# Operand forms in a split-precision MoE kernel: weights at other offsets and in steps, one moving operand in steps, one phase with its columns backwards

## The chip, the cores and the metric

The kernel runs on one core of one Trainium2 chip. The metric is the device time of one execution in microseconds, as the median of several runs. The core has a matrix engine (TensorE: matmuls, and the loads of their weights), a vector engine (VectorE), a scalar engine (ScalarE), GpSimd, and DMA queues, issued here by SyncE. In the profile the engines are PE (with PEld for the weight loads), DVE, ACT, POOL and SP.

## The reference

Sigmoid attention over 8 batches, 12 heads, 448 tokens and 64 dimensions a head, and on its output a two-layer network with a gated activation.

```python
def _attn_ref(q, k, v):
    S = q.shape[2]
    scale = 1.0 / np.sqrt(q.shape[-1])
    scores = scale * np.matmul(q, k.transpose(0, 1, 3, 2)) - np.log(S)
    attn = 1.0 / (1.0 + np.exp(-scores))
    return np.matmul(attn, v).astype(np.float32)

def _moe_ref(x, w_in, w_out):            # x: 3584 x 768, w_in: 768 x 2048, w_out: 2048 x 768
    h = x @ w_in
    relu6 = np.clip(h + 3.0, 0.0, 6.0)
    g = h * relu6 / 6.0
    return (g @ w_out).astype(np.float32)
```

The weights come to the kernel as 8-byte numbers (float64 bits seen as pairs of int32) and are decoded to float32 on the chip.

## The kernel before, in words

The work has three parts in a row on TensorE.

*Attention.* Scores (L200) and attention times values (L217), in quarter-array matmuls of 64 x 64 weights and 448 columns. The other engines meanwhile decode the weights (`decode`, L48 to L66: it reads and writes the low and the high halves of 8-byte numbers, so every second int32) and store them to DRAM.

*The first product, x @ w_in.* It and the second product are done as Strassen-like block products (Winograd's form): seven products M1 to M7 in place of eight, of sums and differences of the quarters of each matrix. `WEIGHT` and `MOVING` name which quarter, or which sum, each product takes as weights and as moving operand. Tokens are taken in four pairs of batches (p = 0 to 3). Each float32 operand is split into a rounded part and a remainder, both in the type float32r (`split`, L69: ScalarE writes the rounded part, VectorE the remainder), and each product of blocks is three matmuls: high by high, high by low, low by high. `w1_split` (L304) splits the weights of one slot: slot n, of 112, has one tile `w_n` of the ring, 128 partitions by two parts of 768 floats, which starts `SHIFT_1` = 48 floats into its buffer. `product` (L362) runs 18 matmuls on it, each with 128 x 128 weights and 448 moving columns. In profiles its rows are L376, with outputs A, B and D.

*The second product, g @ w_out.* The list `units` holds 56 units: for each product in the order of `PHASES` (M1, M2, M6, M7, M5, M4, M3), for each pair p, and for each half h of the inner dimension, one unit of 36 matmuls (three blocks of output rows, four blocks of the inner dimension, three matmuls each; rows of L676, output po). Eight units with the same weights make a phase. Per unit, VectorE forms a difference where the phase needs one (`g_sum`, in M5 and M4), and `g_split` (L479) splits the moving operand into the tile `gx`; this is done two units ahead. `w2_split` (L489) splits a phase's weights, three tiles for each h, of 128 partitions by two parts of 512 floats, `SHIFT_2` = 8 floats into their buffers, one unit ahead. `post2` reads the finished sums. Stores, loads and reloads go through SyncE's queue.

All four engines' orders are written out by the program itself (a manual schedule); the tables `at_slot`, `at_unit` and `at_fetch` set at which slot or unit a step is issued.

The three places where operands get their form:

```python
        w = ring(f"w_{n}", [P, 4 * KW + 64], F32R)[:, SHIFT_1 : SHIFT_1 + 4 * KW]        # w1_split
        gx[n] = gset[n % 3].tile([P, 2, FC, S], F32R, tag="gx", name=f"gx_{n}")          # g_split
            w2[i, h, ec] = w.rearrange("p (t c e) -> p t c e", t=2, c=FC)                # w2_split
```

In all of them each row of 128 weights, or of 448 moving columns, lies in one piece, in rising order, and starts at a multiple of 32 bytes.

Of the kernel before, what the change touches and what calls it, by code (L numbers as in the profile page):

```python
# [9 lines left out]
F32R = mybir.dt.float32r  # L10
# [6 lines left out]
B, H, S, D = 8, 12, 448, 64  # L17
DM, DF = 768, 2048
P = 128
# [6 lines left out]
FC = DF // P // 4  # L26
KW = KC * P
# [5 lines left out]
SHIFT_1, SHIFT_2 = 48, 8  # L33
# [6 lines left out]
M1, M2, M3, M4, M5, M6, M7 = range(7)  # L40
# [2 lines left out]
B11, B21, B22, T4, T1, T2, T3, B12 = range(8)  # L43
MOVING = {M1: B11, M2: B21, M3: B22, M4: T4, M5: T1, M6: T2, M7: T3}
PHASES = (M1, M2, M6, M7, M5, M4, M3)


def decode(nc, st, a):  # L48
# [20 lines left out]
def split(nc, hi, lo, a):  # L69

    nc.scalar.copy(hi, a)  # L71
    yield
    nc.vector.tensor_tensor(out=lo, in0=a, in1=hi.bitcast(F32), op=ALU.subtract)  # L73
    yield
# [20 lines left out]
def tile_kernel(ctx: ExitStack, tc: tile.TileContext, qk, vP, wi, wo, outT):  # L95
    nc = tc.nc
# [44 lines left out]
    def ring(name, shape, dtype):  # L141
        return dw.tile(shape, dtype, tag="ring", name=name, bufs=5)
# [21 lines left out]
    def at_unit(n, f, *a):  # L164
        plan.setdefault(n, []).append((f, a))
# [125 lines left out]
    for u in range(4 * EC):  # L291
        kh, ec = divmod(u, EC)
# [9 lines left out]
            nc.sync.dma_start(out=wst[n], in_=dw1[q % NQ][:, WEIGHT[i]])  # L302

    def w1_split(n):  # L304
        w = ring(f"w_{n}", [P, 4 * KW + 64], F32R)[:, SHIFT_1 : SHIFT_1 + 4 * KW]
        wr[n] = w.rearrange("p (t j c f) -> p t j c f", t=2, j=2, c=KC)
        flat = w.rearrange("p (t n) -> p t n", t=2)
        yield from split(nc, flat[:, 0], flat[:, 1], wst.pop(n).rearrange("p j n -> p (j n)"))
# [10 lines left out]
    for n in range(LA):  # L319
        on(NS - 10 + n, w1_load, n)  # L320
        gen = w1_split(n)
        over(on, (NS - 3 + n,), gen)
        over(on_late, (NS - 2 + n,), gen)
# [127 lines left out]

    units = [(i, p, h) for i in PHASES for p in range(NPR) for h in range(2)]
    gset, gr, gs, gx = [], {}, {}, {}
# [6 lines left out]
    def g_load(n):  # L460
        if n < len(units):
            i, p, h = units[n]
            first, _ = PARTS.get(MOVING[i], (MOVING[i], None))
            gr[n] = gset[n % 3].tile([P, FC, S], F32, tag="gr", name=f"gr_{n}")
            nc.sync.dma_start(out=gr[n], in_=gd[p, first, h])

    def g_load2(n):
        if n < len(units) and MOVING[units[n][0]] in PARTS:
            i, p, h = units[n]
            gs[n] = [ring(f"gr_{n}_{k}", [P, 2, S], F32) for k in range(2)]  # L470
            for k in range(2):
                nc.sync.dma_start(out=gs[n][k], in_=gd[p, PARTS[MOVING[i]][1], h][:, 2 * k : 2 * k + 2])

    def g_sum(n):
        for k, o in enumerate(gs.pop(n, ())):
            part = gr[n][:, 2 * k : 2 * k + 2]
            nc.vector.tensor_tensor(out=part, in0=part, in1=o, op=ALU.subtract)  # L477

    def g_split(n):  # L479
        gx[n] = gset[n % 3].tile([P, 2, FC, S], F32R, tag="gx", name=f"gx_{n}")  # L480
        yield from split(nc, gx[n][:, 0], gx[n][:, 1], gr.pop(n))

    w2s, w2 = {}, {}
# [5 lines left out]
    def w2_split(i, h):  # L489
        st, gens = w2s.pop((i, h)), []  # L490
        for ec in range(EC):
            w = xs.tile(
                [P, KC * S], F32R, tag="xT" if h else "xraw", name=f"w2_{i}_{h}_{ec}", bufs=3 if h else 5
            )[:, SHIFT_2 : SHIFT_2 + 2 * FC * P]
            flat = w.rearrange("p (t n) -> p t n", t=2)
            w2[i, h, ec] = w.rearrange("p (t c e) -> p t c e", t=2, c=FC)
            gens.append(split(nc, flat[:, 0], flat[:, 1], st[:, ec]))
        for _ in range(2):
            for g in gens:
                next(g)  # L500
            yield
# [14 lines left out]
    for n in range(LA, end):  # L516
        over(at_slot, (n - LA, n - LA + 1), w1_split(n))
    for h in range(2):
        at_slot(end - 22 + 7 * h, w2_load, M1, h)
        over(at_slot, (end - 20 + 7 * h, end - 19 + 7 * h), w2_split(M1, h))  # L520
# [9 lines left out]
    at_slot(last[M6, p_last] + 1, xt_close, B11, T2)  # L530
    at_slot(last[M6, p_last] + 1, g_load, 0)
    over(at_slot, (last[M6, p_last] + 3, last[M6, p_last] + 4), g_split(0))
    at_slot(last[M2, p_last] + 1, xt_close, T3, B21)
    at_slot(last[M2, p_last] + 1, g_load, 1)
    over(at_slot, (end, end), g_split(1))
    for n, (i, q) in enumerate(seq):
        for f, a in later.pop(n, []):
# [38 lines left out]
    for h, n in ((0, 0), (1, 8)):  # L576
        for e in range(2 * EC):
            k, ec = divmod(e, EC)
# [8 lines left out]
        at_unit(n + 2 * EC + 2, w2_store, h, S4)  # L587
    for k, i in enumerate(PHASES[1:]):
        n = 8 * (k + 1)
        for h in range(2):  # L590
            if (i, h) == (M6, 1):
                at_unit(n, w2_direct, i, h)
            else:
                at_fetch(n - 2 + h, w2_load, i, h)
            over(at_unit, (n - 1 + h, n - 1 + h), w2_split(i, h))
# [10 lines left out]
    po, so = {}, {}  # L606
# [14 lines left out]
    def post2(i, p, n):  # L621
        t = po.pop(p)
        if n < len(units) - 1:
            t = t[:, :, :S]
        if i == M1:
            so[p] = kept(i, p)
            nc.scalar.mul(so[p], t, SIXTH)
        elif i == M6:
            stt(so[p], t, so[p])
        elif i == M7:  # L630
            so["u3", p] = kept(i, p)
            stt(so["u3", p], t, so[p])
        else:
            eh, k, other = {M2: (0, 0, p), M5: (1, 1, ("u3", p)), M4: (1, 0, ("u3", p)), M3: (0, 1, p)}[i]
            o = out_tile(i, p)
            if n == len(units) - 1:
                for ec in range(EC):
                    stt(o[:, ec], t[ec], so[other][:, ec])
                    nc.sync.dma_start(out=outT[2 * p + k, eh * EC + ec], in_=o[:, ec])
                return  # L640
            stt(o, t, so[other])
            if i == M5:
                stt(so[p], t, so[p])
            at_unit(n + 1, put, p, eh, k, o)

    for n, (i, p, h) in enumerate(units):
        if n == 0:
            for _ in range(2):
                for f, a in later.pop(min(later)):
                    f(*a)  # L650
        elif n == 1:
            while later:
                for f, a in later.pop(min(later)):
                    f(*a)
            tmp_ctx.close()
            acc_ctx.append(ctx.enter_context(tc.tile_pool(name="acc", bufs=1, side="right", reuse_waits="tile")))
        for f, a in fetch.pop(n, []):
            f(*a)
        g_load2(n + 3)
        g_load(n + 4)  # L660
        for f, a in plan.pop(n, []):
            f(*a)
        if n + 2 < len(units):
            g_sum(n + 2)
            for _ in g_split(n + 2):
                pass
        if h == 0 and n == len(units) - 2:
            po[p] = [po_pool.tile([P, 512], F32, tag="pl" if ec < 2 else "po", name=f"pl_{ec}")[:, :S] for ec in range(EC)]
        elif h == 0:
            po[p] = po_pool.tile([P, EC, 512], F32, tag="po", name=f"po_{i}_{p}")  # L670
        x = gx.pop(n)
        for ec in range(EC):
            w = w2[i, h, ec]
            for c in range(FC):
                for wk, xk in ((0, 0), (0, 1), (1, 0)):
                    nc.tensor.matmul(  # L676
                        po[p][ec] if n > len(units) - 3 else po[p][:, ec, :S],
                        w[:, wk, c],
                        x[:, xk, c],
                        start=h == 0 and c == 0 and xk == 0 and wk == 0,  # L680
                        stop=h == 1 and c == FC - 1 and wk == 1,
                    )
        if h == 1:
            post2(i, p, n)
# [34 lines left out]
```

## Time and profile before

| | |
|---|---|
| median of 3 runs | 1074.76 us (1074.35 to 1074.85) |
| the profiled execution | 1075.04 us, span 1073.2 us |
| TensorE busy, matmuls | 1065.8 us, 99% of the span |
| TensorE busy, weight loads | 891.7 us, 83% |
| VectorE, ScalarE, GpSimd busy | 750.0, 561.6, 174.2 us |
| granted TensorE clock | 1.00 |
| DMA queues | 276 MB, 73% of the 16 engines' time |

A group's row gives its line, engine and operation, tiles and shapes and count; then its busy time in us, the mean of one in ns, the idle time of the engine just before its instructions, and what ended most of that. Matmuls are pipelined: the mean of one is longer than the distance between two.

### The profile page before, as it was taken

How to read it: one execution, taken by the hardware profiler on the slowest of the kernel's cores; microseconds unless marked ns; L12 is line 12 of the kernel's file. 1: busy time of each engine (PE TensorE's matmuls, PEld its weight loads, DVE VectorE, ACT ScalarE, POOL GpSimd, SP SyncE). 2: the span in 40 equal slices, each digit the busy share in tenths (PEclk: the TensorE clock that was granted, in tenths of full speed). 3: DMA queues.
4: the chain of work that ended last, by engine and by line, in shares of the span. 5: the costliest groups of instructions: out<-in, count | busy, mean ns of one | idle time of the engine just before them, and what ended most of it. 6: DMA issues, size and time to landing. Idle time of an engine off the chain costs nothing.

```text
span 1073.2 us, 16721 instructions
## 1 busy us (share of the span) xinstructions
PE 1065.8 (99%) x6784; PEld 891.7 (83%) x6784; DVE 750.0 (70%) x713; ACT 561.6 (52%) x612; POOL 174.2 (16%) x82
## 2 busy tenths in 40 slices
PE   9999999999999999999999999999999999999998
PEld 4444556666999999999999999999999999999998
DVE  4679855652677989898988665987864447787642
ACT  7889978886455644665465555434322313222420
POOL 0214230000143236333522221200000000000000
PEclk9999999999999999999999999999999999999999
DMA  8887998873776887779766778878885376898741
GB/s 307 295 323 271 336 362 291 317 276 128 251 252 206 248 280 226 237 229 317 225 216 214 276 248 283 299 265 306 339 315 194 109 276 223 286 345 286 271 149 52
DMA packets 81484, 277.13 MB, mean 258 GB/s; under 512 B 7936, under 2 KB 22272, under 8 KB 81408
## 3 DMA queue, kind: packets, MB, share of 16 engines
q1 hardware_dynamic: 81408, 276.07, 73.3%
q8 instruction: 53, 0.87, 0.3%
q14 instruction: 23, 0.19, 0.0%
HBM read 189.92 MB, written 86.11 MB: 257 GB/s over the span
## 4 chain that ended last, share of the span: by engine, by line
PE 85%; DVE 7%; DMA 3%; ACT 2%; issue 2%; SPq 0%; ACTq 0%; DVEq 0%
PE po L676 26%; PE A L376 21%; PE D L376 11%; PE sc L200 10%; PE pv L217 10%; PE B L376 5%; ACT gx L71 2%; DVE gr L477 2%; PE pl L676 1%; DMA qk<-qk 1%; DMA gr<-gd 1%; DMA dw<-w2S 1%; DVE w L73 1%; DVE gx L73 1%; DVE o L610 0%
## 5 line engine op out<-in xcount | busy, mean ns | idle before, releaser
L676 PE MATMUL po<-gx,w 128*128 128x448 f32 x1944 | 390.0, 362 | 0.6 <-DVE w L73 0.4
L676 PEld LDWEIGHTS po<-gx,w 128*128 128x128 f32 x1944 | 364.1, 187 | 26.4 <-DVE w L73 1.4
L376 PE MATMUL A<-x,w 128*128 128x448 f32 x1152 | 236.1, 362 | 0.4 <-DVE w L73 0.4
L376 PEld LDWEIGHTS A<-x,w 128*128 128x128 f32 x1152 | 215.8, 187 | 15.8 <-DVE w L73 0.7
L71 ACT CAST gx<-gr 128x1792 fp32r<-128x1792 f32 x56 | 94.8, 1694 | 205.0 <-PE po L676 102.4
L200 PE MATMUL sc<-qk 64*64 64x448 f32 x1344 | 197.4, 537 | 1.9 <-DMA qk<-qk 1.0
L217 PE MATMUL pv<-a,v 64*64 64x448 f32 x1344 | 197.1, 536 | 0.0
L202 ACT ACTIVATE a<-sc,bias_s 128x896 f32<-128x896 f32 x168 | 168.6, 1011 | 43.8 <-PE sc L200 39.8
L73 DVE TENSOR_TENSOR w<-ws,w 128x768 fp32r<-128x768 f32 x112 | 155.5, 1397 | 24.9 <-ACT w L71 24.9
L73 DVE TENSOR_TENSOR gx<-gr,gx 128x1792 fp32r<-128x1792 f32 x56 | 113.3, 2024 | 77.2 <-ACT gx L71 77.1
L200 PEld LDWEIGHTS sc<-qk 64*64 64x64 f32 x1344 | 70.3, 133 | 62.8 <-issue 28.3
L217 PEld LDWEIGHTS pv<-a,v 64*64 64x64 f32 x1344 | 71.3, 133 | 59.1 <-issue 38.0
L376 PE MATMUL D<-x,w 128*128 128x448 f32 x576 | 120.3, 362 | 0.0
L71 ACT CAST w<-ws 128x768 fp32r<-128x768 f32 x112 | 93.0, 830 | 43.5 <-DMA ws<-dw 43.4
L376 PEld LDWEIGHTS D<-x,w 128*128 128x128 f32 x576 | 108.0, 187 | 7.2
L228 DVE TENSOR_TENSOR xr<-pv,y 128x448 f32<-128x448 f32 x48 | 29.9, 624 | 79.8 <-ACT y L227 79.8
L410 POOL TENSOR_TENSOR gT<-g,g 128x896 f32<-128x896 f32 x16 | 43.5, 2721 | 258.2 <-DVE g L387 167.1
L376 PE MATMUL B<-x,w 128*128 128x448 f32 x288 | 60.3, 362 | 0.0
L376 PEld LDWEIGHTS B<-x,w 128*128 128x128 f32 x288 | 53.9, 187 | 4.3 <-issue 0.7
L396 ACT ACTIVATE g<-cD,bias 128x896 f32<-128x896 f32 x32 | 33.5, 1047 | 40.8 <-DVE cD L405 24.7
L401 ACT COPY u<-A 128x896 f32<-128x896 f32 x32 | 29.0, 906 | 39.0 <-PE A L376 39.0
L387 DVE SCALAR_TENSOR_TENSOR g<-g,cD 128x896 f32<-128x896 f32 x32 | 43.2, 1351 | 6.3 <-ACT g L396 6.3
(65 smaller groups left out, 766.9 us busy)
## 6 DMA issues: line engine op xcount, KB each, us to landing
gr<-gd SPq DMA_DIRECT2D x56, 896.0 KB, 5.6
ws<-dw SPq DMA_DIRECT2D x112, 384.0 KB, 4.2
gd<-g SPq DMA_DIRECT2D x64, 448.0 KB, 4.8
qk<-qk SPq DMA_DIRECT2D x48, 448.0 KB, 7.1
gd<-gT SPq DMA_DIRECT2D x32, 448.0 KB, 5.2
gr<-gd SPq DMA_DIRECT2D x32, 448.0 KB, 6.0
wi<-wi SPq DMA_DIRECT2D x16, 768.0 KB, 8.4
wo<-wo SPq DMA_DIRECT2D x24, 512.0 KB, 4.5
```

The costliest lines, as they stand in the source:

```text
L71: nc.scalar.copy(hi, a)
L73: nc.vector.tensor_tensor(out=lo, in0=a, in1=hi.bitcast(F32), op=ALU.subtract)
L200: nc.tensor.matmul(out, k[halves[r], at_k], q[halves[r]], start=True, stop=True)
L202: nc.scalar.activation(a, sc[:, :, :S], AF.Sigmoid, bias=bias_s, scale=scale)
L217: nc.tensor.matmul(pv[p][halves[j], r, :S], v, a[halves[r], int(r != j) if c is None else j], start=first, stop=last)
L228: nc.vector.tensor_tensor(out=xr[b, u][:, k], in0=pv[p][:, 1, :S], in1=y, op=ALU.add)
L376: nc.tensor.matmul(t[:, j, :S], w[:, wk, j, kc], x[:, xk, kc], start=i in (M1, M2, M5) and m == 0, stop=m == 3 * KC - 1, skip_group_check= ...
L387: nc.vector.scalar_tensor_tensor(out=r, in0=r, scalar=6.0, in1=h, op0=ALU.min, op1=ALU.mult)
L396: nc.scalar.activation(r, h, AF.Relu, bias=bias_3, scale=1.0)
L401: nc.scalar.copy(acc[key, q], acc["A", q][:, :, :S])
L410: nc.gpsimd.tensor_tensor(out=t3, in0=quad[q, B22], in1=quad[q, B12], op=ALU.subtract)
L676: nc.tensor.matmul(po[p][ec] if n > len(units) - 3 else po[p][:, ec, :S], w[:, wk, c], x[:, xk, c], start=h == 0 and c == 0 and xk == 0 an ...
```

## The change

Some operands of the two products get another form in SBUF or PSUM, each form in a stretch of its own:

- First product: the weights of slot n start n // 14 floats further on. Slots 0 to 13 stay as they are, the next 14 start 4 bytes on, and so on to 28 bytes for the last 14. Each slot has 18 matmuls.
- Second product, phase M6: the weights' tile has its order changed so that the two parts of a weight lie side by side; a row of 128 weights is read in steps of 8 bytes.
- Phase M5: the four inner blocks lie side by side; a row of 128 weights is read in steps of 16 bytes.
- Phase M7, pair 0 alone (units 24 and 25, 72 matmuls): the two parts of the moving operand lie side by side; 448 columns are read in steps of 8 bytes.
- Phase M2: the moving operand's columns are read backwards, and the outputs are written backwards in PSUM, so that each column comes to its old place.

The splits by ScalarE and VectorE write in the new forms, with as many elements and instructions as before. The order of the instructions on every engine is the same before and after; only the listed shape of M6's and M5's weight splits reads 128x4x128 in place of 128x512.

```diff
+BACKWARD = (M2,)
+WEIGHT_FORM = {M6: "p (c e t) -> p t c e", M5: "p (t e c) -> p t c e"}
+INTERLEAVED = (M7, 0)
...
     def w1_split(n):
-        w = ring(f"w_{n}", [P, 4 * KW + 64], F32R)[:, SHIFT_1 : SHIFT_1 + 4 * KW]
+        o = SHIFT_1 + n // 14
+        w = ring(f"w_{n}", [P, 4 * KW + 64], F32R)[:, o : o + 4 * KW]
...
     def g_split(n):
-        gx[n] = gset[n % 3].tile([P, 2, FC, S], F32R, tag="gx", name=f"gx_{n}")
+        t = gset[n % 3].tile([P, 2 * FC * S], F32R, tag="gx", name=f"gx_{n}")
+        form = "p (c s t) -> p t c s" if units[n][:2] == INTERLEAVED else "p (t c s) -> p t c s"
+        gx[n] = t.rearrange(form, t=2, c=FC)
         yield from split(nc, gx[n][:, 0], gx[n][:, 1], gr.pop(n))
...
-            flat = w.rearrange("p (t n) -> p t n", t=2)
-            w2[i, h, ec] = w.rearrange("p (t c e) -> p t c e", t=2, c=FC)
-            gens.append(split(nc, flat[:, 0], flat[:, 1], st[:, ec]))
+            v = w.rearrange(WEIGHT_FORM.get(i, "p (t c e) -> p t c e"), t=2, c=FC)
+            w2[i, h, ec] = v
+            gens.append(split(nc, v[:, 0], v[:, 1], st[:, ec].rearrange("p (c e) -> p c e", c=FC)))
...
+                    out = po[p][ec] if n > len(units) - 3 else po[p][:, ec, :S]
                     nc.tensor.matmul(
-                        po[p][ec] if n > len(units) - 3 else po[p][:, ec, :S],
+                        out[:, ::-1] if i in BACKWARD else out,
                         w[:, wk, c],
-                        x[:, xk, c],
+                        x[:, xk, c, ::-1] if i in BACKWARD else x[:, xk, c],
```

## Prediction

> **What bounds the kernel now.** I read the page first: busy shares, the granted clock, the costliest groups.
>
> ```profile
> span 1073.2 us, 16721 instructions
> PE 1065.8 (99%) x6784; PEld 891.7 (83%) x6784; DVE 750.0 (70%) x713; ACT 561.6 (52%) x612; POOL 174.2 (16%) x82
> PEclk9999999999999999999999999999999999999999
> PE 85%; DVE 7%; DMA 3%; ACT 2%; issue 2%; SPq 0%; ACTq 0%; DVEq 0%
> L676 PE MATMUL po<-gx,w 128*128 128x448 f32 x1944 | 390.0, 362 | 0.6 <-DVE w L73 0.4
> L676 PEld LDWEIGHTS po<-gx,w 128*128 128x128 f32 x1944 | 364.1, 187 | 26.4 <-DVE w L73 1.4
> L376 PEld LDWEIGHTS A<-x,w 128*128 128x128 f32 x1152 | 215.8, 187 | 15.8 <-DVE w L73 0.7
> L200 PEld LDWEIGHTS sc<-qk 64*64 64x64 f32 x1344 | 70.3, 133 | 62.8 <-issue 28.3
> L73 DVE TENSOR_TENSOR w<-w2s,w 128x512 fp32r<-128x512 f32 x39 | 24.5, 685 | 9.1 <-ACT w L71 9.1
> L62 DVE SCALAR_TENSOR_TENSOR wo<-wo 128x512 f32<-128x512 uint32 x24 | 16.6, 692 | 0.7
> ```
>
> TensorE is busy throughout, at the full granted clock, and 85% of the chain that ended last is its matmuls; the other engines have idle time. So the price of an operand's form is what it adds to the distance between two matmuls, not to the 362 ns of one, which overlap. That distance comes from the second product cut into its phases (columns: stretch, its length, then PE, PEld, DVE and ACT busy and the instruction counts, of instructions that touch po).
>
> ```profile
> 664.90:722.50 57.60, 57.60 (x289) 53.99 (x289) 0.00 (x0) 3.89 (x3) 1.00 0.77 289
> 722.50:781.20 58.70, 58.42 (x290) 53.86 (x289) 4.67 (x3) 1.29 (x1) 1.00 0.83 306
> 781.20:838.80 57.60, 57.60 (x289) 53.98 (x289) 6.29 (x5) 0.00 (x0) 1.00 0.66 249
> 838.80:896.40 57.60, 57.60 (x290) 53.99 (x289) 6.16 (x4) 0.00 (x0) 1.00 0.57 205
> 896.40:954.00 57.60, 57.60 (x290) 53.99 (x289) 10.60 (x7) 0.00 (x0) 1.00 0.83 300
> ```
>
> Each phase is 288 matmuls (8 units of 36; an edge adds one or two to the count). 57.60 / 288 = 0.200 us from one matmul to the next. The phases stand here in the order M1, M2, M6, M7, M5.
>
> Does the weight load or the moving stream set the 0.200? The loads look nearly full: 53.99 of 57.60 is 94%, 187 ns of each 200. But one load does not hold its path for 187 ns. That shows at a place where TensorE had run dry and started anew, in the timeline of one third of a microsecond.
>
> ```profile
> 961.86 0.48 PE L676 MATMUL po<-gx,w 128*128 128x448 f32 x1 [0.37 <-DVE w L73]
> 961.86 0.30 PEld L676 LDWEIGHTS po<-gx,w 128*128 128x128 f32 x2 [0.74 <-DVE w L73]
> ```
>
> Two loads of 0.187 fit into 0.30, so the second began 0.30 - 0.187 = 0.11 us after the first: a load holds the path for 0.11, and the rest of its 0.187 is delay. The loads of 64 columns say the same: 187 - 133 = 54 ns for 64 columns more, 0.84 ns a column, 108 ns for 128. The first matmul is recorded 0.48 - 0.36 = 0.12 longer than the others: the wait for its own weights. So a matmul can start about 0.11 after its load, yet matmuls stand 0.200 apart: the moving stream sets the distance, and a load has 0.200 - 0.11 = 0.09 us to spare.
>
> **The change part by part.** No instruction is added, removed or moved; only addresses and steps of operands change.
>
> *Weights of the first product 4 to 28 bytes on.* 112 tiles, the first 14 unchanged, so 98 x 18 = 1764 loads start elsewhere. No row shows a load from such an address. Below, nothing; above, the spare 0.09 covers a load that takes 1.8 times as long. I take 0. ScalarE and VectorE write these tiles at the new addresses: 112 splits, also without a row, taken as 0; in the first product they have 215.0 - 176.1 = 39 us (VectorE) and 90 us (ScalarE) of idle time as cover, and without it a write 5% longer on 155.5 + 93.0 us of splits would cost up to 12.
>
> ```profile
> 430.00:645.00 215.00, 215.00 (x1077) 201.52 (x1076) 176.10 (x140) 124.47 (x142) 62.28 (x21) 1.00 0.75 246
> L73 DVE TENSOR_TENSOR w<-ws,w 128x768 fp32r<-128x768 f32 x112 | 155.5, 1397 | 24.9 <-ACT w L71 24.9
> L71 ACT CAST w<-ws 128x768 fp32r<-128x768 f32 x112 | 93.0, 830 | 43.5 <-DMA ws<-dw 43.4
> ```
>
> *M6's weights in steps of 8 bytes, M5's in steps of 16* (288 loads each). What the trace shows of reading rates, as bytes of address passed over in a nanosecond: a contiguous load passes 512 bytes in 108 ns, 4.7; a contiguous moving operand passes 448 x 4 = 1792 bytes in 200 ns, 9.0. A load in steps of 8 passes 9.5, what the moving read does already: I take 0. A load in steps of 16 passes 19, twice the fastest read in this trace. Bounds: nothing, or double, 0.22 in place of 0.11, which is 0.02 over the 0.200: 288 x 0.02 = 5.8 us. If the load bound after all, doubling would cost 288 x 0.11 = 31.7. I take 0, since a load takes one column in 0.84 ns, half the pace of the moving elements, and may well fetch them singly; the 5.8 stays in the range.
>
> The split instructions write those tiles in steps. VectorE in steps of 8 is in the rows: the decode at L62 reads and writes so, 692 ns against 685 for a contiguous split, so M6's 6 splits cost 6 x 0.007, nothing. Steps of 16 have no row: between 0 and double, 6 x 0.685 = 4.1 us. That is the one place where the cover is thin: in M5 the sums, splits and outputs on VectorE run in an unbroken chain of work up to the stall before 961.86, and M5's first splits stand in it (start, length, what).
>
> ```profile
> 889.32 1.89 DVE w L73 x3
> 891.21 2.02 DVE gr L477 x2
> ...
> 961.21 0.61 DVE w L73
> 961.82 0.04 issue
> 961.86 3.27 PE po L676 x15
> ```
>
> What M5's splits lose comes back there, as a longer wait of TensorE for M4's second weights. I take 0, nearest to the steps-of-8 row, and keep 4.1 as the upper end.
>
> *The moving operand of M7, pair 0, in steps of 8 bytes.* Two units, 72 matmuls. The stream has an element in at most 0.200 / 448 = 0.45 ns, two in the time of one weight column; in steps of 8 it would have to pass 17.9 bytes a nanosecond, twice what any TensorE read does here. Bounds: nothing if elements are fetched singly; double if two neighbours come in one fetch, 72 x 0.200 = 14.4 us. I take the double. This stream sets the distance, so nothing hides it. The reason for the choice is the ratio of two: a read that delivers two elements in a column's time is most simply a read of two neighbours, and this step takes the neighbours apart. The writes of ScalarE and VectorE into these two tiles (in steps of 8, as above) fall into M6, where VectorE is busy 29.04 of 57.60 us: hidden, even doubled.
>
> ```profile
> 781.20:838.80 57.60, 57.60 (x289) 53.98 (x289) 29.04 (x22) 16.74 (x15) 0.00 (x0) 1.00 0.66 249
> ```
>
> *M2 with its columns backwards.* 288 matmuls read x from the last column to the first and write PSUM so. The addresses passed per nanosecond stay, and neighbours stay neighbours, in read and write. Between nothing and double, 288 x 0.200 = 57.6. I take 0.
>
> Sum: 14.4 us. The profiled execution took 1075.04 us (span 1073.2), 0.28 above the median of the runs, 1074.76; from the median, 1089.2.
>
> The Trainium skill prices these steps another way ("Advanced Engine Details and Errata", SBUF Cachelines): lines of 16 bytes, and at least two hits in a line are needed to hide the memory's latency. By that, 4-byte elements in steps of 8 hit a line twice and are free, for the moving operand too, and only M5's weights, one hit in a line, pay: the sum would be 5.8 instead of 14.4. No row of this trace reads anything in steps of 16, and the steps-of-8 rows are VectorE's alone.
>
> **The rivals.**
> - *Everything is hidden* (this ends on the other side, not slower). Each operand has an address generator that takes any step at one element per beat. For it: the decode's 692 against 685, and the 0.09 spare of each load. Against: both are at half the moving operand's pace. It decides at M7's first 72 matmuls: if they stay 0.200 apart, 1074.8 us.
> - *The address span per nanosecond is the limit*, for weights as for the moving operand: 14.4 + 5.8 = 20.2, 1095.0; up to 14.4 + 31.7 = 46.1, 1120.9, if the load were the bound. For it: both forms pass 18 to 19 bytes a nanosecond against a shown 9.0. Against: nothing shows that 9.0 is a limit.
> - *Only the load in steps of 16 pays*: 5.8, 1080.6; with the 4.1 of the split writes 1084.7. For it speaks that the chain through M5 has no slack; against it the 0.09 spare. This is the case of the skill's rule above.
> - *Backwards pays*: 57.6, 1132.4, and with M7 1146.8. It takes a write or a read that pairs neighbours only in rising order; a contiguous trace can't show one. The skill ("PSUM — Partial Sum Buffer", Specifications) says that any non-contiguous access slows matmuls significantly; whether descending neighbours count as such, it does not say, and no row here shows it.
> - *A gain*: a new offset would have to take away waits of TensorE. All its idle time is 1073.2 - 1065.8 = 7.4 us, down to 1067.4, and its stalls are on other engines' writes, which offsets do not bring forward.
>
> **How the numbers follow.** A difference of 0.2% (2.1 us) is about what a measurement of this kernel can tell from none. The moving step pays: 0.42, of which 0.27 alone (1089.2) and 0.15 with the 16-byte weights (1095.0 or more). Everything hidden: 0.34 (1074.8). Only the 16-byte step: 0.06. Backwards: 0.14. A gain: 0.04. The likeliest is that the moving step pays, and in it the plain case, 1089.2; its own range is 1086 to 1096. Slower is 0.42 + 0.06 + 0.14 = 0.62, same 0.34, faster 0.04. The range for 8 in 10 leaves out backwards and the gain (0.18): from 1074, where everything is hidden, to 1121, the span limit with the load as the bound.
>
> **What would show it.** The matmuls of M7's first two units 0.40 us apart, the other six units 0.200; the phase 14 us longer and everything behind it later by as much. M6 and the first product at 0.200 with loads of 187 ns. M5: 57.6 us, and the wait before M4's second weights no more than the present 0.4. M2: 57.6 us and its stalls as now. The forecast is wrong if M7's pair 0 keeps 0.200, if a load of M5 is recorded above some 275 ns, or if M2's distance grows.

## The result, and the profile after

| | before | after |
|---|---|---|
| median, in runs on the same chip | 1074.8 us (1074.35 to 1075.67) | 1107.35 us (1107.04 to 1107.82) |
| ratio | | 1.0301, 95% interval 1.0288 to 1.0314 |
| profiled span | 1073.2 us | 1105.8 us |

The change costs 32.6 us, 2.3 times the forecast's 14.4: inside the range of 1074 to 1121, but outside the 1086 to 1096 that the forecast's own case had. The page of the changed kernel, the lines that answer to those of before (L683 is the second product, L380 the first):

```profile
span 1105.8 us, 16721 instructions
PE 1099.5 (99%) x6784; PEld 907.8 (82%) x6784; DVE 753.1 (68%) x713; ACT 565.0 (51%) x612; POOL 174.1 (16%) x82
PEclk9999999999999999999999999999999999999999
L683 PE MATMUL po<-gx,w 128*128 128x448 f32 x1944 | 416.1, 377 | 0.3 <-ACT w L74 0.2
L683 PEld LDWEIGHTS po<-gx,w 128*128 128x128 f32 x1944 | 381.1, 210 | 35.2 <-issue 13.6
L380 PE MATMUL A<-x,w 128*128 128x448 f32 x1152 | 239.9, 365 | 0.4 <-DVE w L76 0.4
L380 PEld LDWEIGHTS A<-x,w 128*128 128x128 f32 x1152 | 216.3, 188 | 19.1 <-DVE w L76 0.7
```

TensorE is as busy as before, at the same clock, and waits for nobody more than before: its matmuls stand farther apart. The second product's phases show where (stretch, length, PE, PEld, DVE and ACT busy and counts, of instructions on po). In order: M1, M2, M6, M7 pair 0, M7 pairs 1 to 3, M5, M4.

```profile
671.55:729.15 57.60, 57.60 (x288) 54.02 (x288) 0.00 (x0) 3.89 (x3) 1.00 0.77 288
729.15:789.49 60.34, 60.04 (x290) 53.92 (x288) 4.67 (x3) 1.29 (x1) 1.00 0.83 300
789.49:848.05 58.56, 58.56 (x290) 55.91 (x288) 6.23 (x4) 0.00 (x0) 1.00 0.65 242
848.05:876.59 28.54, 28.54 (x74) 14.98 (x72) 1.56 (x1) 0.00 (x0) 1.00 0.20 73
876.59:919.82 43.23, 43.23 (x217) 40.54 (x216) 4.68 (x3) 0.00 (x0) 1.00 0.62 226
919.82:987.02 67.20, 67.20 (x289) 67.19 (x289) 10.61 (x7) 0.00 (x0) 1.00 0.76 275
987.02:1044.62 57.60, 57.60 (x289) 54.01 (x288) 7.68 (x5) 0.00 (x0) 1.00 0.78 279
```

M7's pair 0 takes 28.54 / 72 = 396 ns a matmul, M5 67.20 / 288 = 233.3, M6 58.56 / 288 = 203.3; M1, M4 and the rest of M7 keep 200. In M5 the loads are now busy without a gap (67.19 of 67.20). M2's matmuls stand 206.7 apart; the rest of its 60.34 are waits that it had before.

The first product's stretches of 14 slots, 252 matmuls each, by how far the weights are moved: 4, 8, 12, 16, 20, 24, 28 bytes (instructions that touch w). Before, each of these stretches took 50.40 us; the last row shows the first of them.

```profile
311.99:363.23 51.24, 51.24 (x253) 47.46 (x252) 17.57 (x14) 11.63 (x14) 1.00 0.66 208
363.23:413.67 50.44, 50.44 (x254) 47.30 (x252) 23.17 (x14) 11.65 (x14) 1.00 0.86 276
413.67:464.91 51.24, 51.24 (x253) 47.36 (x252) 21.50 (x14) 11.61 (x14) 1.00 0.68 214
464.91:516.43 51.52, 51.52 (x253) 47.31 (x252) 22.70 (x14) 11.64 (x14) 1.00 0.85 275
516.43:569.07 52.64, 52.64 (x253) 47.55 (x252) 22.06 (x15) 11.63 (x14) 1.00 0.65 204
569.07:620.31 51.24, 51.24 (x253) 47.31 (x252) 18.72 (x18) 13.25 (x17) 1.00 0.72 245
620.31:671.55 51.24, 51.24 (x253) 47.31 (x252) 13.44 (x14) 10.71 (x14) 1.00 0.73 247
311.93:362.33 50.40, 50.40 (x253) 47.24 (x252) 17.62 (x14) 11.59 (x14) 1.00 0.69 211
```

Next to nothing at 8 bytes (0.2 ns a matmul), 3.3 at 4, 12, 24 and 28, 4.4 at 16, 8.9 at 20, while a load is recorded at 188 ns in place of 187. The splits that write these tiles cost what they cost before: 1393 ns on VectorE and 832 on ScalarE, against 1397 and 830.

The difference of the two traces, stretch by stretch (for before, from the starts of the same matmuls):

| part | forecast | measured |
|---|---|---|
| first product, offsets | 0 | +6.8 us (411.8 against 405.1) |
| M2, backwards | 0 | +1.9 |
| M6, weights in steps of 8 | 0 | +0.8 (1.0 less a wait of before) |
| M7 pair 0, moving operand in steps of 8 | +14.4 | +14.1 |
| M5, weights in steps of 16 | 0 (bound 5.8) | +9.6 |
| M4, waits at its start | 0 | -0.7 |
| sum | +14.4 | +32.5 of 32.6 |

The one term of the forecast came; 18.4 of the 32.5 us came from terms that it had at nothing.

### The profile page after: what moved, and what is told of

It reads as the page before. It is cut to its first block, busy times and chain, and to the rows that moved or that the text cites. A ratio compares the mean times of both kernels' runs of the same rounds, so it can differ in the third digit from the quotient of the medians.

```text
span 1105.8 us, 16721 instructions
## 1 busy us (share of the span) xinstructions
PE 1099.5 (99%) x6784; PEld 907.8 (82%) x6784; DVE 753.1 (68%) x713; ACT 565.0 (51%) x612; POOL 174.1 (16%) x82
## 4 chain that ended last, share of the span: by engine, by line
PE 95%; DMA 2%; DVE 1%; issue 1%; ACT 1%; SPq 0%; ACTq 0%; DVEq 0%
PE po L683 35%; PE A L380 21%; PE sc L203 11%; PE D L380 11%; PE pv L220 10%; PE B L380 5%; DMA qk<-qk 2%; PE pl L683 1%; DMA dw<-w2S 1%; PE idle L334 0%; DVE w L76 0%; DVE gx L76 0%; ACT a L205 0%; DVE w2S L566 0%; DVE w L567 0%
## 5 line engine op out<-in xcount | busy, mean ns | idle before, releaser
L683 PE MATMUL po<-gx,w 128*128 128x448 f32 x1944 | 416.1, 377 | 0.3 <-ACT w L74 0.2
L683 PEld LDWEIGHTS po<-gx,w 128*128 128x128 f32 x1944 | 381.1, 210 | 35.2 <-issue 13.6
L380 PE MATMUL A<-x,w 128*128 128x448 f32 x1152 | 239.9, 365 | 0.4 <-DVE w L76 0.4
L380 PEld LDWEIGHTS A<-x,w 128*128 128x128 f32 x1152 | 216.3, 188 | 19.1 <-DVE w L76 0.7
L76 DVE TENSOR_TENSOR w<-ws,w 128x768 fp32r<-128x768 f32 x112 | 155.1, 1393 | 23.7 <-ACT w L74 23.6
L380 PE MATMUL D<-x,w 128*128 128x448 f32 x576 | 122.4, 365 | 0.0
L380 PEld LDWEIGHTS D<-x,w 128*128 128x128 f32 x576 | 108.3, 188 | 8.9
L380 PE MATMUL B<-x,w 128*128 128x448 f32 x288 | 61.3, 366 | 0.0
L380 PEld LDWEIGHTS B<-x,w 128*128 128x128 f32 x288 | 54.1, 188 | 5.1 <-issue 0.7
L409 DVE TENSOR_TENSOR cD<-D,u 128x896 f32<-128x896 f32 x32 | 34.8, 1087 | 19.0 <-ACT u L405 10.9
```

The source lines that it names most:

```text
L380: nc.tensor.matmul(t[:, j, :S], w[:, wk, j, kc], x[:, xk, kc], start=i in (M1, M2, M5) and m == 0, stop=m == 3 * KC - 1, skip_group_check= ...
L409: nc.vector.tensor_tensor(out=c, in0=acc[name, q][:, :, :S], in1=acc[key, q], op=ALU.add)
L683: nc.tensor.matmul(out[:, ::-1] if i in BACKWARD else out, w[:, wk, c], x[:, xk, c, ::-1] if i in BACKWARD else x[:, xk, c], start=h == 0 ...
```

## The experiments

Two theories stood at the start for the parts that I had at nothing: a read is priced by its own form (start, step, direction), or two reads that run at once, weights and moving operand, get in each other's way. For M5 the question was whether the load itself binds. A time without a ratio is that of one execution. Distances are those between the starts of successive matmuls in its trace, waits left out.

**One part alone: the offsets.**

```diff
-        w = ring(f"w_{n}", [P, 4 * KW + 64], F32R)[:, SHIFT_1 : SHIFT_1 + 4 * KW]
+        o = SHIFT_1 + n // 14
+        w = ring(f"w_{n}", [P, 4 * KW + 64], F32R)[:, o : o + 4 * KW]
```

> The kernel before with the one part 'weights of the first product 4 to 28 bytes on'. In the trace of the changed kernel a slot of 18 matmuls lasts 3.60 us at offsets of 0 and 8 bytes, 3.66 at 4, 12, 24 and 28, 3.68 at 16 and 3.76 at 20. If that is the price of the offsets themselves, the seven stretches of 14 slots cost 14 x (0.06 + 0 + 0.06 + 0.08 + 0.16 + 0.06 + 0.06) = 6.7 us here too: 1081.5 us. If it needs another part of the change (other timing of the engines that write the tiles, other addresses elsewhere), this kernel stays within 2 us of 1074.8.

Measured 1081.63 us against 1075.29, ratio 1.0058 (1.0042 to 1.0075). The first product took 411.8 us, as in the changed kernel, against 405.1 before: the 6.8 us of the table are the offsets' own, and no other part of the change is needed for them.

**Both operands moved, the weights by phase, the moving operand by pair** (in floats; before: 8 and 0).

```diff
+W_AT = {M1: 8, M2: 9, M6: 10, M7: 11, M5: 12, M4: 13, M3: 0}
+X_AT = (0, 1, 4, 5)
...
-        gx[n] = gset[n % 3].tile([P, 2, FC, S], F32R, tag="gx", name=f"gx_{n}")
+        t = gset[n % 3].tile([P, 2 * FC * S + 16], F32R, tag="gx", name=f"gx_{n}")
+        o = X_AT[units[n][1]]
+        gx[n] = t[:, o : o + 2 * FC * S].rearrange("p (t c s) -> p t c s", t=2, c=FC)
...
-            )[:, SHIFT_2 : SHIFT_2 + 2 * FC * P]
+            )[:, W_AT[i] : W_AT[i] + 2 * FC * P]
```

> The kernel before, with only the second product's operands moved: the weights of each phase by their own offset (M1 as before, M2 4 bytes on, M6 8, M7 12, M5 16, M4 20, M3 32 bytes back), and the moving operand of each pair by its own (pair 0 as before, pairs 1, 2, 3 by 4, 16 and 20 bytes). Theory 1, the weights' own address sets the price: the distance of two matmuls is the same in all four pairs of a phase, 200, 203.3, 200, 203.3, 204.4, 208.9 ns in M1, M2, M6, M7, M5, M4 (as in the first product at these offsets), in all 5.8 us. Theory 2, two reads that run at once get in each other's way, so that the difference of the two addresses counts: pair 0 as in theory 1, but 200 ns wherever both moved alike (M2 pair 1, M5 pair 2, M4 pair 3), and M1 itself slower in the pairs whose moving operand moved (203 to 209 ns).

1086.35 us; both theories missed as stated. Weights 4 bytes on (M2) gave 203 ns in pair 0, whose moving operand has no offset, but 200.0 in the first unit of pair 2, whose moving operand is 16 bytes on: the weights' own address does not set the price. Nor does the difference alone: with both 16 bytes on (M5, first unit of pair 2) it is as before, and the distance is 206.6. And M1's pair 0, where no offset was changed, came to 200 in one half and 204 in the other: the tile, enlarged by 16 floats, had shifted the second of the three buffers by 64 bytes (and the third by 128, so only every third unit has the plain offsets).

```profile
665.42:672.62 7.20, 7.20 (x36) 6.75 (x36) 0.00 (x0) 0.00 (x0) 1.00 1.01 364
672.62:680.00 7.38, 7.38 (x38) 6.80 (x37) 0.00 (x0) 0.00 (x0) 1.00 0.92 339
```

The two rows are those units, 36 matmuls each (the second's stretch has a few ns of the next). So whole multiples of 32 bytes matter too, and the next run takes only those.

**Starts at multiples of 32 bytes only.** As the last kernel, with the tile enlarged by 128 floats so that every buffer starts at the same place modulo 512 bytes, and

```diff
+W_AT = {M1: 0, M2: 8, M6: 16, M7: 24, M5: 32, M4: 40, M3: 48}
+X_AT = (0, 8, 16, 24)
```

> The kernel before, second product: weights of the phases M1, M2, M6, M7, M5, M4, M3 at 0, 32, 64, 96, 128, 160, 192 bytes past a multiple of 128 (before: 32 everywhere), the moving operand of pairs 0 to 3 moved by 0, 32, 64, 96 bytes (before: 0, which is 96 past a multiple of 128). All starts are multiples of 32 bytes. Theory 1, only starts off 32 bytes cost: 200 ns everywhere, 1074.8 us. Theory 2, two reads meet in the memory and the distance of their addresses, modulo 128, counts: equal prices along equal distances, 200 at 64 (M2 pair 0, M6 pair 1, M7 pair 2), and 204 to 205 at others, as the runs before had 204 at a distance of 0 and 205 at 32: up to 5 us longer.

1081.52 us. Distance of two matmuls in ns, the mean over a pair's two units, by how many bytes, modulo 256, the weights start past the moving operand:

| weights less moving start | 0 | 32 | 64 | 96 | 128 | 160 | 192 | 224 |
|---|---|---|---|---|---|---|---|---|
| ns, in each phase and pair at this distance | 202.6, 206.5, 206.7, 206.7 | 204.4, 204.4, 204.5 | 202.1, 202.1, 202.2 | 200.1, 200.2, 206.6 | 203.9, 204.0, 204.0 | 205.3 (four times) | 200.0 (four times) | 206.5, 206.5, 204.4, 204.4 |

Five distances of eight have one value each, though phase, pair, buffers and everything around differ; three have two. Theory 1 falls: all these starts are multiples of 32, and 200 to 207 ns come out. Theory 2 is the nearer one, with the period at 256 bytes, not 128 (64 and 192 differ), but not as a clean function. Rows of M7, pairs 0 to 3 (14.40 is the undisturbed time), and M5's pair 0:

```profile
841.36:855.94 14.58, 14.58 (x73) 13.52 (x72) 1.56 (x1) 0.00 (x0) 1.00 0.37 128
855.94:870.81 14.87, 14.87 (x73) 13.54 (x72) 1.56 (x1) 0.00 (x0) 1.00 0.36 125
870.81:885.21 14.40, 14.40 (x73) 13.50 (x72) 1.56 (x1) 0.00 (x0) 1.00 0.81 300
885.21:899.99 14.78, 14.78 (x73) 13.52 (x72) 1.56 (x1) 0.00 (x0) 1.00 0.70 259
899.99:914.71 14.72, 14.72 (x74) 13.51 (x73) 1.55 (x1) 0.00 (x0) 1.00 0.64 220
```

The kernel before has a distance of 192 in both products (by the addresses that the compiled program gives its tiles), one of the two at which matmuls stood 200 apart; in the first product it lost that with every offset but 8.

**Shorter loads at such distances.** In the kernel before, with the weights' start as in the second experiment:

```diff
+W_AT = {M1: 0, M2: 0, M6: 16, M7: 16, M5: 24, M4: 24, M3: 48}
+ROWS = (128, 96, 64, 32)
...
+                    rows = ROWS[p] if c in (1, 2) else P
...
-                        po[p][ec] if n > len(units) - 3 else po[p][:, ec, :S],
-                        w[:, wk, c],
+                        (po[p][ec] if n > len(units) - 3 else po[p][:, ec, :S])[:rows],
+                        w[:, wk, c, :rows],
```

> The kernel before; in the second product the weights' start is moved so that the distance from the moving operand's start to the weights', modulo 256 bytes, is 160 in M1 and M2, 224 in M6 and M7, 0 in M5 and M4, 96 in M3 (192 before). In the run with aligned starts these distances gave 205.3; 204.4 or 206.6; 202.6 or 206.7; 200.0 or 206.6 ns. The two middle inner blocks use 128, 96, 64, 32 columns of weights in pairs 0 to 3 (so products lack part of their rows). Theory 1, the weights' read disturbs the moving read while both run: what is above 200 falls with the load's length, to three quarters, a half and a quarter (in M1 and M2 from 5.3 to 4.0, 2.7, 1.3 ns). Theory 2, something happens once at each change of weights, by the addresses: it stays at 5.3 at any number of columns. Pair 0 repeats the earlier run's values if they are a function of the addresses alone.

Distances between two cut matmuls in pairs 0 to 3 (in pair 0 nothing is cut): M6 and M7 206.5, 204.3, 202.6, 200.0; M1 and M2 205.4, 202.3, 203.9, 200.2; M5 and M4 206.6, 202.7, 203.0, 205.0; M3 206.6, 202.2, 201.4, 203.9. M6's four pairs, two units each, half of whose matmuls are cut:

```profile
782.10:796.96 14.86, 14.86 (x74) 13.53 (x72) 1.55 (x1) 0.00 (x0) 1.00 1.00 395
796.96:811.68 14.72, 14.72 (x74) 12.54 (x72) 1.56 (x1) 0.00 (x0) 1.00 0.61 220
811.68:826.32 14.64, 14.64 (x74) 11.61 (x72) 1.56 (x1) 0.00 (x0) 1.00 0.49 178
826.32:840.92 14.60, 14.60 (x74) 10.64 (x72) 1.56 (x1) 0.00 (x0) 1.00 0.50 181
```

In M6 and M7 the excess falls nearly with the load's length (6.5, 4.3, 2.6, 0.0); in M1 and M2 it ends at nothing but not evenly; in the last three phases it falls and comes back. So theory 2 is out (the load's length matters everywhere), and theory 1 fits one pair of starts alone. Pair 0 repeats the aligned run in M1, M2, M6 and M7, but not in M3: with the same offsets, and so the same starts modulo 256 bytes, its pair 0 takes 206.6 here and took 200.1 there. So the two starts modulo 256 do not fix the price either. That the two reads meet in the memory is the reading that fits; no run shows it, and a rule that gives the number beforehand I do not have.

**Moving operand moved, by 0 to 6 floats from phase to phase, forwards and backwards.**

```diff
+        t = gset[n % 3].tile([P, 2 * FC * S + 128], F32R, tag="gx", name=f"gx_{n}")
+        o = PHASES.index(units[n][0])
...
+                        out[:, ::-1] if p > 1 else out,
...
+                        x[:, xk, c, ::-1] if p > 1 else x[:, xk, c],
```

> The kernel before, second product: the moving operand starts 0, 4, 8, 12, 16, 20, 24 bytes on in the phases M1, M2, M6, M7, M5, M4, M3; pairs 0 and 1 read forwards, pairs 2 and 3 backwards with backward outputs. The weights stay where they are. Theory 1, the moving read alone costs it, through a start inside a 32-byte piece: forwards 200 in M1 and 206.7 in the others; backwards the first element is 1788 bytes on, 28 past a multiple of 32, so 206.7 in all phases but M2, where it is at a multiple of 32. Theory 2, the price comes from meeting the weights' read and has no such order: values from 200 to 209, backward ones not equal to each other. By theory 1 some 5.8 + 0.96 = 7 us longer, 1082.

1087.29 us. Forwards, at 0 to 24 bytes: 200.1, 207.8, 204.9, 200.8, 203.3, 220.0, 204.6. Backwards: 206.7 in six phases and 210.0 at 8 bytes. So neither theory for all of it: the forward read goes by where it starts, as in the runs above, and the backward read costs 6.7 almost wherever it starts. M4 (20 bytes), pairs 0 and 1 forwards, 2 and 3 backwards:

```profile
961.26:977.07 15.81, 15.81 (x73) 13.82 (x72) 3.02 (x2) 0.00 (x0) 1.00 0.64 218
977.07:992.91 15.84, 15.84 (x73) 13.82 (x72) 1.55 (x1) 0.00 (x0) 1.00 0.91 331
992.91:1007.80 14.89, 14.89 (x74) 13.68 (x73) 1.55 (x1) 0.00 (x0) 1.00 0.72 258
1007.80:1022.68 14.88, 14.88 (x74) 13.68 (x73) 1.56 (x1) 0.00 (x0) 1.00 0.78 278
```

**Backwards: the read or the write?**

```diff
+                        out[:, ::-1] if i in (M6, M7) else out,
...
+                        x[:, xk, c, ::-1] if i in (M2, M7) else x[:, xk, c],
```

> The kernel before, with the moving operand read backwards in M2, the output written backwards in M6, and both in M7 (so M2 and M6 put their columns in the wrong order). In the changed kernel both at once cost 6.7 ns a matmul. Theory 1, the write to PSUM costs it: M2 200, M6 206.7, M7 206.7 ns. Theory 2, the read costs it: M2 206.7, M6 200, M7 206.7. A share each: M2 and M6 around 203. By theories 1 and 2 the time is 1074.8 + 576 x 0.0067 = 1078.6 us.

1078.26 us. M2's last three pairs (216 matmuls, read backwards), M6 (written backwards), M7 (both):

```profile
738.10:782.74 44.64, 44.64 (x218) 40.55 (x216) 4.67 (x3) 0.00 (x0) 1.00 0.78 284
782.74:840.34 57.60, 57.60 (x290) 54.01 (x289) 6.22 (x4) 0.00 (x0) 1.00 0.66 248
840.34:899.85 59.51, 59.51 (x289) 54.06 (x288) 6.23 (x4) 0.00 (x0) 1.00 0.55 200
```

206.7, 200 and 206.6 ns: the read pays all of it, the write to PSUM nothing.

**Larger steps.** The changed kernel without offsets and backward reads, with

```diff
-WEIGHT_FORM = {M6: "p (c e t) -> p t c e", M5: "p (t e c) -> p t c e"}
-INTERLEAVED = (M7, 0)
+WEIGHT_FORM = {M6: "p (c e t) -> p t c e", M5: "p (t e c) -> p t c e", M4: "p (e c t) -> p t c e"}
+MOVING_FORM = {(M7, 0): "p (c s t) -> p t c s", (M7, 1): "p (t s c) -> p t c s"}
...
```

> The changed kernel without offsets and without the backward phase, and with two larger steps: the moving operand of M7 in steps of 8 bytes in pair 0 (as there) and of 16 bytes in pair 1, the weights in steps of 8 bytes in M6, 16 in M5 (as there) and 32 in M4. Theory 1, a read fetches neighbours together, and once they are apart nothing more is lost: pair 1 as pair 0, 397 ns a matmul; M4 as M5, 233 ns and loads of 330 ns; in all 1074.8 + 14.1 + 14.1 + 1.0 + 9.6 + 9.6 = 1123 us. Theory 2, the addresses passed in a nanosecond are the limit: pair 1 twice pair 0, some 770 ns (+ 41 us), M4's loads twice as long, above 450 ns a matmul (+ 70 us or more), in all over 1190 us.

1126.14 us. M7's pair 0 (steps of 8) and 1 (steps of 16), M5 (weights in steps of 16), M4 (in steps of 32):

```profile
839.44:867.98 28.54, 28.54 (x73) 14.98 (x72) 1.56 (x1) 0.00 (x0) 1.00 0.21 73
867.98:897.02 29.04, 29.04 (x73) 15.01 (x72) 1.56 (x1) 0.00 (x0) 1.00 0.26 95
925.86:993.06 67.20, 67.20 (x289) 67.20 (x289) 10.61 (x7) 0.00 (x0) 1.00 0.77 275
993.06:1063.13 70.07, 70.07 (x289) 70.06 (x289) 7.68 (x5) 0.00 (x0) 1.00 0.66 233
```

396 and 403 ns; 233 and 243 ns. As theory 1 had it, a step twice as large then costs only 2% and 4% more. The addresses passed in a nanosecond are not the limit, which was the forecast's second rival. That a read fetches neighbours together fits these rows, but they show only where the rate drops: at 8 bytes for the moving operand, and for the weights between 8 (M6, next run) and 16.

**Is M5 bound by its load? Fewer moving columns.** The changed kernel with only the weights' steps:

```diff
+CUT = (384, 320, 256, 192)
...
+                    cols = CUT[p] if c and i in (M1, M6, M5) else S
...
+                        out[:, :cols],
...
+                        x[:, xk, c, :cols],
```

> The changed kernel without offsets, backward phase and moving steps; in M1 (contiguous weights), M6 (steps of 8 bytes) and M5 (steps of 16) the matmuls of three of the four inner blocks stream fewer columns: 384, 320, 256, 192 in pairs 0 to 3 (so those products lack part of their columns). Question: is M5's 233 ns the weight load, or a slower moving stream? Theory 1, the load sets it: M5 keeps 233 ns at every number of columns, while M1 falls by 0.42 ns a column (173, 147, 120, 93 ns) until its own load of 110 to 120 ns stops it in the last one or two pairs; M6 the same, 3 ns above. Theory 2, the stream is slowed where it meets the load: M5 falls too, by 27 ns for each 64 columns (206, 180, 153). And if the record of 187 ns were the time that a contiguous load needs, M1 would stay at 200 throughout.

Three quarters of a unit's 36 matmuls are cut. First three rows: M1, pairs 0, 1, 2; last four: M5, pairs 0 to 3; two units each.

```profile
665.03:677.99 12.96, 12.96 (x72) 12.73 (x72) 0.00 (x0) 0.00 (x0) 1.00 1.00 356
677.99:689.52 11.53, 11.53 (x73) 11.29 (x73) 0.00 (x0) 1.30 (x1) 1.00 0.68 239
689.52:699.25 9.73, 9.73 (x74) 9.50 (x73) 0.00 (x0) 1.30 (x1) 1.00 0.85 335
884.94:901.71 16.77, 16.77 (x73) 16.77 (x73) 1.55 (x1) 0.00 (x0) 1.00 0.53 181
901.71:918.49 16.78, 16.78 (x74) 16.78 (x73) 3.02 (x2) 0.00 (x0) 1.00 0.84 301
918.49:935.26 16.77, 16.77 (x74) 16.77 (x73) 3.02 (x2) 0.00 (x0) 1.00 0.81 301
935.26:952.03 16.77, 16.77 (x74) 16.77 (x73) 3.02 (x2) 0.00 (x0) 1.00 0.87 315
```

With the 18 whole ones of two units at 0.200, M1's cut matmuls stand (12.96 - 3.6) / 54 = 173, 147 and 113.5 ns apart; at 192 columns the single distances were 111, no longer falling by 27. M5 takes 16.77 with every cut: 16.77 / 72 = 233 ns, whatever streams. Theory 1, without remainder: a contiguous load of 128 columns holds its path for about 110 ns, as read from the 0.30 us row before the change; one in steps of 16 bytes holds it for 233. M6's load is not the bound at 448 columns: its cut matmuls fell to 175, 149 and 120, and stayed at 120 with 192 columns, so a load in steps of 8 holds its path for about 120.

**The other side: fewer weight columns.** Again the changed kernel, without offsets and moving steps:

```diff
+ROWS = (128, 96, 64, 32)
...
+                    rows = ROWS[p] if c in (1, 2) and i in (M2, M6, M5) else P
...
+                        (out[:, ::-1] if i in BACKWARD else out)[:rows],
+                        w[:, wk, c, :rows],
```

> The changed kernel without offsets and moving steps; in M2 (moving operand backwards), M6 (weights in steps of 8) and M5 (steps of 16) the matmuls of the two middle inner blocks use 128, 96, 64, 32 columns of weights in pairs 0 to 3 (so those products lack part of their rows). Theory 1: M5's load is the bound, so with 96 columns, whose load takes three quarters, its matmuls are back at 200 ns; M2's 6.7 ns come from the moving read itself and stay at any number of weight columns. Theory 2, reads that meet slow the stream: M5 loses its 33 ns in proportion (25, 17, 8 ns above 200), M2 its 6.7 (5, 3.3, 1.7).

M5's cut matmuls stand 233, 206, 204 and 201 ns apart; their loads, by number of columns (behind the bar the busy time in us, then the mean of one in ns):

```profile
L685 PEld LDWEIGHTS po<-gx,w 128*128 128x128 f32 x73 | 17.1, 330 | 0.0
L685 PEld LDWEIGHTS po<-gx,w 128*96 128x96 f32 x36 | 7.8, 255 | 0.0
L685 PEld LDWEIGHTS po<-gx,w 128*64 128x64 f32 x36 | 7.1, 196 | 0.3
L685 PEld LDWEIGHTS po<-gx,w 128*32 128x32 f32 x36 | 5.0, 139 | 2.0
```

With 96 columns the load no longer binds (theory 1), but 6, 4 and 1 ns stay that theory 1 did not have, of the size of the address effects above. From 96 to 32 columns the recorded time falls by 116 ns for 64 columns, 1.81 a column; 128 x 1.81 = 232, close to the 233. M2's backward 6.7 became 4.8, 4.5 and 4.8: neither constant nor in proportion; open. M6's 3.3 became 5.2, 2.8 and 1.4: it too changes with the load's length, and not evenly.

**M5's step alone, and its writes alone.**

The changed kernel with the offsets out and

```diff
-BACKWARD = (M2,)
-WEIGHT_FORM = {M6: "p (c e t) -> p t c e", M5: "p (t e c) -> p t c e"}
-INTERLEAVED = (M7, 0)
+BACKWARD = ()
+WEIGHT_FORM = {M5: "p (t e c) -> p t c e"}
+INTERLEAVED = None
```

> The kernel before with M5's weights in steps of 16 bytes alone. Theory: the load holds its path for 233 ns and sets M5's distance, 288 x 33.3 ns = 9.6 us; the wait before M4's second weights goes, since VectorE and ScalarE get 9.6 us more in M5 (-0.6 us): 1083.8 us. Rival: part of the 9.6 us comes from other parts of the change, and this kernel is nearer to the forecast's own bound of 5.8: 1080.6.

1083.71 us against 1074.77, ratio 1.0079 (1.0062 to 1.0096), as the theory had it (1083.8).

And the kernel before, whose matmuls go on reading the tile as it was:

```diff
-            gens.append(split(nc, flat[:, 0], flat[:, 1], st[:, ec]))
+            v = w.rearrange("p (t e c) -> p t c e" if i == M5 else "p (t c e) -> p t c e", t=2, c=FC)
+            gens.append(split(nc, v[:, 0], v[:, 1], st[:, ec].rearrange("p (c e) -> p c e", c=FC)))
```

> The kernel before, with M5's weights written in steps of 16 bytes but read contiguously, as before (so M5's products are taken with weights in the wrong places). In the changed kernel such a write took VectorE 1.09 us in place of 0.685 and ScalarE 1.15 in place of 0.62. Theory 1, the prediction's thin cover: the chain on VectorE through M5 has no slack, so 6 x 0.4 = 2.4 us come back in the wait before M4's second weights: 1077.2 us. Theory 2: the chain waits in between for other things that do not move (data from DRAM, finished sums of TensorE), and the time stays within 1 us of 1074.8. M5's matmuls stay at 200 ns by both.

1079.6 us (1077.89 to 1080.0), ratio 1.0038 (1.0023 to 1.0053). The group of VectorE's six splits of M5, and TensorE's longest wait:

```profile
L73 DVE TENSOR_TENSOR w<-w2s,w 128x512 fp32r<-128x512 f32 x6 | 6.1, 1079 | 0.0
```

```profile
PE po L676 <- DVE w L73: 2.7, 1, 2.7
```

Three stretches behind that wait, which ended at 965.25 (TensorE alone; the third column from the end is the granted clock):

```profile
966.00:967.00 1.00, 1.00 (x4) 0.50 1.05 405
967.00:968.00 1.00, 1.00 (x5) 0.50 1.06 360
969.00:970.00 1.00, 1.00 (x7) 1.00 0.84 315
```

A split on VectorE that reads the rounded part and writes the remainder in steps of 16 takes 1079 ns in place of 685. That makes 6 x 0.39 = 2.4 us, and 2.3 of them come back in the wait before M4's second weights, 0.4 before, 2.7 now: theory 1. M5 keeps 57.6 us. More came than was counted: for some 3.5 us after the wait the granted clock was 0.50, and matmuls stood 373 ns apart, which cost 1.7 us more. The phase of M4 is 3.9 us longer by both; the other 1.0 of this execution was lost before the second product began. Of the four executions the one whose granted clock stayed at 1.000 took 1077.89 us, near the 1077.2 of theory 1; the three at 0.997 and 0.998 took 1079.25 to 1080.0.

## Why the prediction was wrong, point by point

Two steps failed above all: the load of M5's weights, put at nothing under a bound of 5.8 us, cost 9.6, and the offsets of the first product, put at nothing without a row, cost 6.8. M2 and M6, also at nothing, cost 1.9 and 0.8. The time lies inside the forecast's range only because that range reached up to a span limit, which the run with larger steps refuted; that is luck.

*What bounds the kernel: right.* The moving stream sets the 0.200 us, and a contiguous load holds its path for about 0.11: the cut columns showed it at 111 ns. The rival that the load's record of 187 ns is the bound is refuted by M1's 147 ns.

*M7's moving operand: right,* 14.1 us against 14.4, and the reason given fits: a step that parts neighbours doubles, a larger one adds 2%, a backward read, which keeps neighbours together, adds 3%. The Trainium skill's rule ("Advanced Engine Details and Errata", SBUF Cachelines), by which 4-byte elements in steps of 8 would be free, does not hold for this read.

*M5's weights: the step that failed most in size.* I took 0 and bounded the load at double, 0.22 us; it is 233 ns, more than twice 110, and 33 ns a matmul show. "May well fetch them singly" was an argument without a row. The sign named beforehand, a load of M5 recorded above some 275 ns, came: 330. Here the same rule of the Trainium skill (one hit in a line pays) had the right operand.

*The weights' offsets: the step that failed in kind.* "The spare 0.09 covers a load that takes 1.8 times as long" priced the load's length, and the length did not change. What changed was where it reads, and by the runs on both operands' starts that counts together with where the moving operand reads; the distance of the matmuls grows, and it has no spare at all. That the two reads meet is inferred, and which starts cost how much stays open. No row of before could show it: all its operands stand at one distance, 192 bytes modulo 256. The upper bound of zero was therefore not a bound.

*M2 backwards: mis-sized,* 1.9 us of 0 to 57.6, with its distance grown, which was named as a sign beforehand; the read pays, 6.7 ns, not the write. The Trainium skill's sentence ("PSUM — Partial Sum Buffer", Specifications) that any non-contiguous access slows matmuls significantly showed nothing for descending columns: M6 written backwards kept 57.60 us.

*M6: mis-sized,* 3.3 ns a matmul, 1.0 us; its load, recorded 194 in place of 187 and holding its path for about 120, does not bind. Of the cause only that is shown, and that the 3.3 change with the load's length.

*The split writes: the thin cover was rightly named.* 2.4 us were lost on VectorE and 2.3 came back as a wait, as the rows of the chain said, within the bound of 4.1; in the changed kernel they are free because M5 itself grew by 9.6 us, and M4's wait went (-0.7). Alone they cost 4.1 us by the ratio (2.5 to 5.7); the profiled execution has 3.9 in M4's phase: the wait, and the lower clock behind it, for which the forecast had no term.

*Two readings of rows.* The rows with steps of 8 are not VectorE's alone: ScalarE too reads the high halves so in the decode (L52, 674 ns for 128 x 512, against 617 for a contiguous split). And the decode's 692 ns for 512 elements are a third of the moving operand's pace, not half. Neither changes the sum.

*The chances.* The cases were drawn as if one operand paid, or two by one common limit, and the rest were free. Five forms paid at once, each a little to a lot; no case held that sum.

## What to carry to other kernels

A zero for a hidden resource has to be bounded by what it shares with the bound one, not only by its own spare time: a weight load with half its time free still came with a stream 2 to 10% slower, by the addresses of the two. For matmuls at full rate, keep float32r operands contiguous and in rising order when read (descending output columns cost nothing here), and when tiles move in a pool, compare the matmul distance before and after: 64 bytes more in one tile cost 4 ns a matmul here. A form to be priced is best put into one phase of a kernel with a neighbour phase as control, since each stretch then reads its own price to a tenth of a nanosecond.

## What the runs showed of the hardware that I had not expected

- The distance of two matmuls depends on both operands' start addresses: 200.0 to 206.7 ns among starts at multiples of 32 bytes, up to 220 with the moving operand 20 bytes on. At five of eight differences modulo 256 the value is one, at three there are two, and the same starts modulo 256 gave 200.1 in one run and 206.6 in another; what chooses is open.
- Weights in steps of 16 bytes load at 1.81 ns a column (233 ns for 128), in steps of 8 in about 120 ns for 128, contiguous ones in about 111.
- A moving operand in steps of 8 runs at half rate, 396 ns; in steps of 16 hardly slower, 403.
- Splits into float32r in steps of 16 bytes took VectorE 1090 ns (it reads one part so and writes the other) against 685, and ScalarE, which only writes so, 1150 against 617, for 128 x 512; in steps of 8, ScalarE 690 and VectorE 685.
- After a wait of TensorE of 2.7 us the granted clock was 0.50 for some 3.5 us (matmuls 373 ns apart), then 1.00 again.
